# The second layers of an eight-expert block, with the loop over products put outside the loop over experts

## The chip, the cores and the metric

The kernel runs on 1 core of one Trainium2 chip. The metric is device time in microseconds, of which the median of 3 runs is shown. A profile of one execution gives the rows of this document.

## What is computed

A local and a pooled attention give x (2304 tokens by 512); a dense block follows; then a block of eight experts, each token weighted by a matrix P that is balanced over tokens and experts:

```python
h = np.maximum(x @ w_in, 0.0)
x = h * h @ w_out
...
for e in range(E):                     # E = 8
    h = np.maximum(x @ w1[e], 0.0)     # 512 -> 1024
    ye = h @ w2[e]                     # 1024 -> 512
    out += P[:, e:e + 1] * ye
```

All is in float32.

## The kernel before

All instructions are written by generators that an ordering loop (class `Order`) runs against estimated costs; the order in which it takes them is the order of each engine's queue, and each queue runs in that order. All loads and stores are issued by SP, in one queue. Buffers are rings of tiles; a generator that asks for a tile (`get`) waits until one is put back.

Both layers of the experts use seven products instead of eight for a two-by-two split of each matrix multiplication: tokens are taken in three pairs of blocks `pb` of 2 x 384, and the weight and the hidden matrix in halves. Sums and differences of quarters of the weights, and of the hidden matrix, are multiplied. Each float32 operand is split into a high and a low part (`split2`, lines 464 to 468: ScalarE writes the high part at line 466, VectorE or GpSimd the low part at line 468), and a product takes three matmuls of 128x384.

The first layers (`l1_second`, line 1376 for the matmuls) leave, for each expert and pair, the seven hidden combinations in DRAM (`scr_h`). Six units of expert 0 are computed before P is known; they are stored raw (`scr_c`), and `later` (lines 1499 to 1542) loads them in the second layers, multiplies them by P on VectorE (line 1527), forms the combinations (line 1532) and stores them. `later` starts at step 7 of the second layers and goes on by one step for each of its DMAs (`PACE`). Expert 0 is therefore the last of `EXPERTS`.

The second layers are 168 steps (`l2_second`, lines 1608 to 1632): for each expert, each pair and each product, in this order, 24 matmuls into two banks (line 1624). `hidden_loads` (1588) loads each hidden combination in two halves of 384 KB (tiles r); `hidden` (1601) splits a half into a tile of the ring `s_h` (tiles xa, h, i). `l2_weights` (1549) loads the four quarters of an expert's weights once, forms four sums (1575, 1582) and splits seven operands into the ring `s_w` (tiles w, v, u). `collect` (1638) adds each of a step's two banks to an accumulator in SBUF: for the first expert a copy by ScalarE (1647), for the others an add by VectorE (1651). There are 21 accumulators, one for each pair and product. After the last expert `finish` (1655) combines a pair's seven accumulators by seven adds (1663), transposes them (1679), copies them (ScalarE, 1681) and stores 768 KB for each block (1685).

`room` (1191 to 1223) hands out SBUF as the first layers release it: to `s_h` one, four and one tiles, to `s_raw` four.

## Time and profile before

| | |
|---|---|
| median of 3 runs | 2044.64 us (2039.79 to 2044.87) |
| the profiled execution, its own time | 2043.14 us |
| its span, first to last instruction | 2041.4 us |
| mean granted TensorE clock | 0.983 |
| TensorE matmul, VectorE, ScalarE, GpSimd busy | 96%, 76%, 44%, 31% |
| mean DMA rate over the span | 219 GB/s |

PE is TensorE's matmuls, PEld its weight loads, DVE VectorE, ACT ScalarE, POOL GpSimd, SP the engine that issues the DMAs. An "L" and a number is a line of the kernel. In the chain that ended last, each piece is what released the next.

### The profile page before, as it was taken

The page shows a single profiled execution, that of the slowest core. Times are in us where ns is not written, and L with a number is a line of the kernel's source. Part 1 is how long each engine was busy: PE and PEld are TensorE (multiplying, and loading weights), DVE is VectorE, ACT ScalarE, POOL GpSimd, SP SyncE. Part 2 cuts the span into 40 slices and gives each one's busy share as a digit, 9 for nine tenths or more (in the row PEclk, how much of TensorE's full clock was granted, in tenths as well). Part 3 has the DMA queues.
Part 4 walks back from the last instruction along what each step waited for, and adds up shares of the span by engine and source line. Part 5 has one row for each costly group of instructions (what it writes and reads, how often), then busy time and mean ns, then how long its engine had stood idle before and what let it go on. Part 6 is the DMA issues. An engine that isn't in the chain of part 4 may idle for free.

```text
span 2041.4 us, 30758 instructions
## 1 busy us (share of the span) xinstructions
PE 1964.4 (96%) x11201; PEld 1853.8 (91%) x11201; DVE 1542.9 (76%) x2157; ACT 891.6 (44%) x1601; POOL 626.2 (31%) x416
## 2 busy tenths in 40 slices
PE   8899999999989999999999999899999999999997
PEld 5577777899979999999999999898988999999997
DVE  7998988681264777777777777868878787978885
ACT  4575545566633222222222222664434454444543
POOL 4444031002003333333333332023333352534441
PEclk8899999999989999999999999999999999999998
DMA  7667676566475666666666666887876767577664
GB/s 211 213 228 221 209 203 195 157 217 209 138 258 181 234 224 222 234 226 227 224 237 227 218 243 224 300 262 224 248 239 203 269 213 250 179 226 227 194 202 139
DMA packets 244848, 446.84 MB, mean 219 GB/s; under 512 B 22440, under 2 KB 144856, under 8 KB 244696
## 3 DMA queue, kind: packets, MB, share of 16 engines
q1 hardware_dynamic: 244696, 444.87, 67.1%
q8 instruction: 88, 1.44, 0.3%
q14 instruction: 64, 0.52, 0.1%
HBM read 280.61 MB, written 164.18 MB: 218 GB/s over the span
## 4 chain that ended last, share of the span: by engine, by line
PE 79%; DVE 9%; DMA 7%; issue 2%; ACT 2%; POOL 1%; SPq 1%; DVEq 0%; ACTq 0%; POOLq 0%
PE b L1376 33%; PE b L1624 31%; PE b L992 6%; PE b L1033 6%; DMA o<-in_w_in_dram 1%; DMA r<-scr_h 1%; DMA lk<-in_kp_dram 1%; DVE f L922 1%; DVE xa L468 1%; DVE f L924 1%; DVE lp L851 1%; DMA x<-scr_x 1%; DMA o<-in_w_out_dram 1%; DMA lk<-in_vp_dram 0%; DMA xa<-scr_x 0%
## 5 line engine op out<-in xcount | busy, mean ns | idle before, releaser
L1376 PE MATMUL b<-x,w 128*128 128x384 f32 x2688 | 497.4, 338 | 6.3 <-DMA x<-scr_x 5.3
L1376 PEld LDWEIGHTS b<-x,w 128*128 128x128 f32 x2688 | 469.6, 188 | 7.9 <-issue 5.0
L468 DVE TENSOR_TENSOR xa<-r,xa 128x768 fp32r<-128x768 f32 x210 | 260.3, 1253 | 63.1 <-ACT xa L466 62.4
L466 ACT ACTIVATE xa<-r 128x768 fp32r<-128x768 f32 x224 | 189.5, 846 | 243.5 <-DMA r<-scr_h 136.1
L1624 PE MATMUL b<-xa,w 128*128 128x384 f32 x1232 | 263.4, 337 | 5.4 <-DVE xa L468 5.4
L1376 PE MATMUL b<-xa,w 128*128 128x384 f32 x1344 | 263.7, 339 | 3.0 <-DMA xa<-scr_x 3.0
L1376 PEld LDWEIGHTS b<-xa,w 128*128 128x128 f32 x1344 | 238.5, 190 | 4.6 <-DMA xa<-scr_x 3.7
L1624 PEld LDWEIGHTS b<-xa,w 128*128 128x128 f32 x1232 | 219.6, 189 | 6.8 <-DVE xa L468 6.7
L468 POOL TENSOR_TENSOR w<-w,w 128x1024 fp32r<-128x1024 f32 x71 | 158.6, 2234 | 191.8 <-ACT w L466 191.7
L1624 PE MATMUL b<-xa,u 128*128 128x384 f32 x736 | 186.6, 337 | 3.1 <-DVE xa L468 3.1
L1443 ACT ACTIVATE b<-b 128x384 f32<-128x384 f32 x96 | 45.6, 475 | 322.2 <-PE b L1376 320.5
L1624 PE MATMUL b<-xa,v 128*128 128x384 f32 x720 | 167.9, 342 | 5.7 <-DVE v L468 5.7
L1449 ACT ACTIVATE q<-b 128x384 f32<-128x384 f32 x192 | 93.5, 491 | 180.0 <-PE b L1376 149.6
L1033 PE MATMUL b<-g,s 128*128 128x512 f32 (+1 forms) x756 | 168.9, 369 | 0.9 <-ACT t L1058 0.9
L1033 PEld LDWEIGHTS b<-g,s 128*128 128x128 f32 x756 | 135.9, 188 | 17.9 <-ACT t L1058 1.5
L1230 POOL TENSOR_TENSOR w<-w 128x256 f32<-128x256 f32 x64 | 55.0, 859 | 309.3 <-PE b L1376 258.7
L992 PE MATMUL b<-x,s 128*128 128x512 f32 (+1 forms) x600 | 138.7, 374 | 4.8 <-DVE g L1011 3.8
L1624 PEld LDWEIGHTS b<-xa,u 128*128 128x128 f32 x736 | 134.0, 188 | 4.0 <-DVE xa L468 4.0
L1624 PEld LDWEIGHTS b<-xa,v 128*128 128x128 f32 x720 | 131.7, 192 | 6.1 <-DVE v L468 6.1
L1409 DVE SCALAR_TENSOR_TENSOR q<-q,gp 128x768 f32<-128x768 f32 x90 | 125.1, 1390 | 3.1
L1473 DVE TENSOR_TENSOR q<-b,q 128x384 f32<-128x384 f32 x96 | 53.5, 557 | 95.9 <-PE b L1376 95.8
L992 PEld LDWEIGHTS b<-x,s 128*128 128x128 f32 x600 | 107.8, 190 | 20.0 <-DVE g L1011 5.0
(255 smaller groups left out, 3296.5 us busy)
## 6 DMA issues: line engine op xcount, KB each, us to landing
r<-scr_h SPq DMA_DIRECT2D x336, 384.0 KB
scr_h<-q SPq DMA_DIRECT2D x90, 576.0 KB
scr_h<-q SPq DMA_DIRECT2D x180, 192.0 KB
scr_h<-q SPq DMA_DIRECT2D x90, 384.0 KB
s<-scr_w SPq DMA_DIRECT2D x85, 256.0 KB
w<-in_w_dram SPq DMA_DIRECT2D x64, 256.0 KB
gp<-scr_p SPq DMA_DIRECT2D x30, 384.0 KB
m<-scr_w SPq DMA_DIRECT2D x43, 256.0 KB
```

Source lines behind the costliest of these rows:

```text
L466: A.activation(out=hi, in_=x, func=AF.Copy)
L468: eng.tensor_tensor(out=lo_, in0=x, in1=hi.bitcast(F32), op=ALU.subtract)
L851: V.tensor_tensor(out=pr.rearrange("p r s d -> p (r s) d"), in0=sc[:, i].unsqueeze(2).to_broadcast([128, r * W, D]), in1=_free(v[:, :, :], ...
L992: PE.matmul(ps[:, 0:n], lhsT=w[:, a, c], rhs=x[:, b, 0:n], start=(cc == 0 and i == 0), stop=(cc == 3 and i == 2))
L1033: PE.matmul(acc[dc][:, 0:n], lhsT=w[:, a, c], rhs=g[:, b, 0:n], start=(fc == 0 and i == 0), stop=(fc == NF - 1 and i == 2))
L1230: eng.tensor_tensor(out=out, in0=in0, in1=in1, op=op)
L1376: PE.matmul(bank[:, 0:TN], lhsT=w[a][:, iw % 4, cc * 128:cc * 128 + 128], rhs=x[:, b, cc], start=(first and cc == 0 and i == 0), stop=(cc ...
L1409: V.scalar_tensor_tensor(out=x, in0=x, scalar=0.0, in1=p.unsqueeze(1).to_broadcast([128, 2, TN]), op0=ALU.max, op1=ALU.mult)
L1443: A.activation(out=ps[1][:, 0:TN], in_=ps[0][:, 0:TN], func=AF.Copy)
L1449: A.activation(out=c[:, place], in_=ps[bank][:, 0:TN], func=AF.Copy)
L1473: V.tensor_tensor(out=c[:, 2], in0=ps[0][:, 0:TN], in1=c[:, 2], op=ALU.add)
L1624: PE.matmul(ps[d][:, 0:TN], lhsT=w[a][:, q, d * 128:d * 128 + 128], rhs=h[:, b, q % 2], start=(q == 0 and m == 0), stop=(q == NQ - 1 and m ...
```

## The change

Products become the outer loop and experts the inner one. The 168 steps stay; their order is a table, `PASSES`: products 1, 2 and 4 (`PUT_OFF`) for experts 1 to 7 and all pairs; then products 1, 2 and 4 for expert 0; then products 5, 6, 3 and 7 for all eight experts. The products of all experts of one pair are added up in the two banks of that pair, so that six banks are held through a product. `collect` runs once for each pair and product (for the first three products a second time, for expert 0), and adds the banks into two accumulator blocks `u` and `c` of the pair, or straight into an output block, which `turned` transposes, copies and stores in two pieces (256 KB and 128 KB); `finish` is gone.

Weights are loaded for each product and expert: one quarter for products 1, 2 and 4, two for 5 and 7, three for 6, one for 3. The sum formed for product 5 and the one formed for product 6 are stored to DRAM (`scr_s`) and loaded again for products 6 and 3. The sums and low parts of the weights go to GpSimd less readily (1000 ns instead of 3000). `later` starts at step 2, goes on by two steps at fewer places, and not beyond step 50. The ring `s_h` gets five tiles and five more of `s_q`; `s_raw` gets the three tiles of `s_p` when `later` is through; `s_w` gets 18 tiles instead of 19.

```diff
-PRODUCTS = (1, 2, 4, 6, 5, 3, 7)
+PRODUCTS = (1, 2, 4, 5, 6, 3, 7)
-PACE = 1
+PUT_OFF, PACE = (1, 2, 4), 2
 ...
-        s_w.add(slots(p, 4, [128, 4, 256], "u"))
-        s_h.add(slots(p, 1, [128, 4, TN], "i"))
-        s_acc.add(slots(p, 3, [128, 4, TN], "y"))
+        s_w.add(slots(p, 3, [128, 4, 256], "u"))
+        s_h.add(slots(p, 5, [128, 4, TN], "i"))
         yield ("need", lambda: not any(gleft.values()) and len(s_q.idle) == NX2)
-        s_acc.add(s_q)
+        s_h.add(*s_q.all)
+        yield ("need", lambda: len(s_p.idle) == NP2)
+        s_raw.add(*s_p.all)
 ...
-        yield ("need", lambda: at2["step"] >= 7)
+        yield ("need", lambda: at2["step"] >= 2)
-            n = at2["step"] + PACE
+            n = min(at2["step"] + PACE, 50)
 ...
+    PASSES = [(k, pb, e) for k in PUT_OFF for e in EXPERTS[:-1] for pb in range(NPB)]
+    PASSES += [(k, pb, LAST) for k, pb in ((1, 0), (1, 1), (2, 0), (1, 2), (2, 1), (2, 2))]
+    PASSES += [(k, pb, LAST) for k in PUT_OFF[2:] for pb in range(NPB)]
+    PASSES += [(k, pb, e) for k in rest for e in EXPERTS for pb in range(NPB)]
+    TERMS = {1: ((0, 0),), 2: ((1, 0),), 4: ((1, 1),), 5: ((0, 1), (1, 1)), 6: ("S1", (0, 0), (1, 0)), 3: ("S4",),
+             7: ((0, 1), (0, 0))}
 ...
     def l2_weights():
-        for e in EXPERTS:
-            for d, f in ((0, 0), (0, 1), (1, 1), (1, 0)):
-                dma(out=a[f, d], in_=w12[e, f:NF2:2, :, 1, d * 256:(d + 1) * 256].rearrange("q p c -> p q c"))
+        for k, e in WEIGHTS:
+            for term in TERMS[k]:
+                x = yield get(s_w)
+                if (term, e) in scr_s:
+                    dma(out=x, in_=scr_s[term, e])
+                else:
+                    dma(out=x, in_=w12[e, f:NF2:2, :, 1, d * 256:(d + 1) * 256].rearrange("q p c -> p q c"))
+            order.add(weight2(e, k, a, hi, lo_), 8.0)
+    def weight2(e, k, a, hi, lo_):
+        late = 0.0 if k == PRODUCTS[0] else 1000.0
 ...
+        if k == 5:
+            yield from two(x, x, a[1], ALU.add)
+            yield from keep("S1", x)
+        elif k == 6:
+            yield from two(x, x, a[1], ALU.subtract)
+            yield from two(a[2], a[2], x, ALU.subtract)
+        elif k == 7:
+            yield from two(x, a[1], x, ALU.subtract)
+        yield from split2(x, NQ * 256, hi, lo_, late)
+        if k == 6:
+            yield from keep("S4", a[2])
 ...
     def l2_second():
+        for k, pb, e in PASSES:
+            first, last = e == EXPERTS[0] or more and not on, e == LAST or k in PUT_OFF and e == EXPERTS[-2]
 ...
+                            PE.matmul(ps[pb][d][:, 0:TN], lhsT=w[a][:, q, d * 128:d * 128 + 128], rhs=h[:, b, q % 2],
+                                      start=(first and q == 0 and m == 0), stop=(last and q == NQ - 1 and m == 2),
+                                      skip_group_check=True)
+            if last:
+                order.add(collect(pb, k, ps[pb], more), 1.2)
 ...
+    def collect(pb, k, ps, more):
+        for d in range(2):
+            if k == 1 and not more:
+                A.activation(out=u[:, d], in_=ps[d][:, 0:TN], func=AF.Copy)
+            for x, of in adds:
+                V.tensor_tensor(out=x[:, d], in0=ps[d][:, 0:TN], in1=of[:, d], op=ALU.add)
+            for x, of, _, _ in outs:
+                V.tensor_tensor(out=x[:, d], in0=ps[d][:, 0:TN], in1=x[:, d] if of is None else of[:, d], op=ALU.add)
+    def turned(x, t0, d0):
+        for t, n in ((0, 2), (2, 1)):
+                    PE.transpose(ps[:, i * 256 + d * 128:i * 256 + d * 128 + 128], x[:, d, c], ident)
+            dma(out=out[t0 + t * 128:t0 + (t + n) * 128, d0:d0 + 256].rearrange("(t p) d -> p t d", p=128), in_=o[:, t:t + n])
```

Three places show how the change moves instructions. The first is VectorE's queue in the early second layers. Before, from the second expert on (xa, i, h on line 468 are low parts of hidden halves, b a bank, xa on line 1651 an accumulator):

```order
L468 TENSOR_TENSOR xa_1973_13656<-r_1969_13625,xa_1973_13656 128x768
L468 TENSOR_TENSOR xa_1978_13680<-r_1970_13634,xa_1978_13680 128x768
L1651 TENSOR_TENSOR xa_1820_12809<-b_1974_13657,xa_1820_12809 128x384
L1651 TENSOR_TENSOR xa_1820_12809<-b_1975_13663,xa_1820_12809 128x384
L468 TENSOR_TENSOR i_1980_13698<-r_1972_13648,i_1980_13698 128x768
L468 TENSOR_TENSOR h_1987_13723<-r_1976_13671,h_1987_13723 128x768
L1651 TENSOR_TENSOR xa_1820_12809<-b_1981_13699,xa_1820_12809 128x384
L1651 TENSOR_TENSOR xa_1820_12809<-b_1985_13707,xa_1820_12809 128x384
L468 TENSOR_TENSOR xa_1990_13742<-r_1979_13690,xa_1990_13742 128x768
L468 TENSOR_TENSOR xa_1994_13764<-r_1986_13714,xa_1994_13764 128x768
L1651 TENSOR_TENSOR xa_1836_12896<-b_1991_13743,xa_1836_12896 128x384
L1651 TENSOR_TENSOR xa_1836_12896<-b_1992_13748,xa_1836_12896 128x384
```

Now, in the first product (u and w are low parts of weights):

```order
L468 TENSOR_TENSOR i_1805_12796<-r_1804_12786,i_1805_12796 128x768
L468 TENSOR_TENSOR i_1807_12807<-r_1806_12797,i_1807_12807 128x768
L468 TENSOR_TENSOR q_1809_12818<-r_1808_12808,q_1809_12818 128x768
L468 TENSOR_TENSOR u_1812_12830<-w_1802_12771,w_1811_12829 128x1024
L468 TENSOR_TENSOR h_1814_12854<-r_1810_12826,h_1814_12854 128x768
L468 TENSOR_TENSOR xa_1816_12865<-r_1815_12855,xa_1816_12865 128x768
L468 TENSOR_TENSOR xa_1818_12875<-r_1817_12866,xa_1818_12875 128x768
L468 TENSOR_TENSOR xa_1820_12889<-r_1819_12876,xa_1820_12889 128x768
L468 TENSOR_TENSOR w_1823_12901<-v_1813_12831,v_1822_12900 128x1024
L468 TENSOR_TENSOR q_1825_12912<-r_1821_12894,q_1825_12912 128x768
```

The two adds of each step are gone from between the splits, and low parts of weights stand there instead.

The second place is SP's queue about step 112 of 168 (r and gp are raw hidden halves, w, v and u weight tiles, scr_S the weight sums in DRAM). Before:

```order
L1598 DMA r_2538_16892<-scr_h_0_161 128x768
L1598 DMA r_2545_16926<-scr_h_0_161 128x768
L1598 DMA r_2546_16936<-scr_h_1_162 128x768
L1598 DMA r_2553_16968<-scr_h_1_162 128x768
L1598 DMA r_2556_16983<-scr_h_1_162 128x768
L1567 DMA u_2558_16991<-in_w_dram 128x4x256
L1598 DMA r_2560_17012<-scr_h_1_162 128x768
L1598 DMA r_2565_17030<-scr_h_1_162 128x768
L1567 DMA w_2561_17014<-in_w_dram 128x4x256
```

Now, while products of kind 6 are multiplied:

```order
L1581 DMA u_2388_16490<-in_w_dram 128x4x256
L1627 DMA r_2391_16517<-scr_h_0_161 128x768
L1597 DMA scr_S_7_182<-v_2365_16348 128x1024
L1627 DMA r_2395_16537<-scr_h_1_162 128x768
L1578 DMA w_2397_16542<-scr_S_1_176 128x1024
L1627 DMA r_2399_16564<-scr_h_1_162 128x768
L1578 DMA v_2402_16569<-scr_S_2_177 128x1024
L1627 DMA gp_2404_16586<-scr_h_2_163 128x768
L1627 DMA gp_2407_16608<-scr_h_2_163 128x768
L1597 DMA scr_S_0_175<-u_2388_16490 128x1024
```

The loads of weights stand closer, and stores and loads of weight sums stand between the hidden loads; the last store shown writes the tile that the first row loads.

The third place is the end of VectorE's queue. Before, after the last product's matmuls (q are accumulators):

```order
L1651 TENSOR_TENSOR q_1914_13314<-b_2943_19299,q_1914_13314 128x384
L1651 TENSOR_TENSOR q_1914_13314<-b_2945_19305,q_1914_13314 128x384
L1663 TENSOR_TENSOR q_1862_13057<-q_1862_13057 128x768
L1663 TENSOR_TENSOR q_1879_13143<-q_1862_13057,q_1879_13143 128x768
L1663 TENSOR_TENSOR q_1879_13143<-q_1879_13143 128x768
L1663 TENSOR_TENSOR q_1862_13057<-q_1879_13143,q_1898_13230 128x768
L1663 TENSOR_TENSOR q_1898_13230<-q_1862_13057,q_1898_13230 128x768
L1663 TENSOR_TENSOR q_1898_13230<-q_1862_13057,q_1914_13314 128x768
L1663 TENSOR_TENSOR q_1879_13143<-q_1879_13143,q_1914_13314 128x768
```

Now (i are two output blocks, b the last two banks):

```order
L1697 TENSOR_TENSOR i_2720_18953<-b_2645_18215,xa_1890_13300 128x384
L1697 TENSOR_TENSOR i_2721_18954<-b_2645_18215,xa_1890_13300 128x384
L1697 TENSOR_TENSOR i_2720_18953<-b_2646_18221,xa_1890_13300 128x384
L1697 TENSOR_TENSOR i_2721_18954<-b_2646_18221,xa_1890_13300 128x384
```

Of the last step's two adds from banks and seven sums, four adds from banks are left.

## Rows read from the trace of the kernel before

**Rows 1.** Page, busy time by engine over the span
```profile
PE 1964.4 (96%) x11201; PEld 1853.8 (91%) x11201; DVE 1542.9 (76%) x2157; ACT 891.6 (44%) x1601; POOL 626.2 (31%) x416
```

**Rows 2.** Page, the chain that ended last, by line
```profile
PE b L1376 33%; PE b L1624 31%; PE b L992 6%; PE b L1033 6%; DMA o<-in_w_in_dram 1%; DMA r<-scr_h 1%; DMA lk<-in_kp_dram 1%; DVE f L922 1%; DVE xa L468 1%; DVE f L924 1%; DVE lp L851 1%; DMA x<-scr_x 1%; DMA o<-in_w_out_dram 1%; DMA lk<-in_vp_dram 0%; DMA xa<-scr_x 0%
```

**Rows 3.** Stretches: us, then PE, PEld, DVE, ACT, POOL busy (xinstructions), PEclk, DMA share, GB/s
```profile
1280.00:1320.00 40.00, 34.27 (x180) 33.67 (x179) 34.49 (x41) 24.79 (x36) 0.00 (x0) 0.91 0.83 284
1320.00:1380.00 60.00, 60.00 (x347) 60.00 (x346) 38.35 (x36) 40.00 (x61) 13.29 (x5) 1.00 0.85 270
1380.00:1420.00 40.00, 34.92 (x185) 33.30 (x185) 34.93 (x38) 15.81 (x21) 16.99 (x6) 0.96 0.66 211
...
1480.00:1520.00 40.00, 35.83 (x202) 34.68 (x201) 30.69 (x38) 15.45 (x18) 15.96 (x7) 1.00 0.69 220
...
1560.00:1620.00 60.00, 52.72 (x286) 50.78 (x285) 49.45 (x57) 22.94 (x28) 21.67 (x9) 0.97 0.66 220
...
1700.00:2000.00 300.00, 300.00 (x1731) 299.78 (x1730) 246.56 (x279) 144.41 (x171) 122.59 (x49) 1.00 0.69 212
```

**Rows 4.** Waits of PE, 1285:2025 us
```profile
PE b L1624 <- DVE xa L468: 8.5, 7, 3.3
PE b L1624 <- DVE v L468: 5.7, 1, 5.7
```

**Rows 5.** Chain in order of time, 1272:1680 us: start us, us, what
```profile
1283.46 5.78 DMA r<-scr_h
...
1292.18 0.95 DVE h L468
1293.13 1.15 DVE v L468
```

**Rows 6.** The same view, 1380:1420 us
```profile
1392.52 0.56 DVE y L1651 x2
...
1395.02 2.26 DVE xa L468
...
1399.03 5.23 DVE xa L468 x2
...
1404.28 3.44 DMA r<-scr_h
...
1409.69 2.37 POOL w L468
```

**Rows 7.** DVE and POOL groups, 1700:2000 us: xcount | busy us, mean ns | idle before
```profile
L468 DVE TENSOR_TENSOR xa<-r,xa 128x768 fp32r<-128x768 f32 x87 | 116.6, 1357 | 23.4 <-ACT xa L466 23.0
...
L1651 DVE TENSOR_TENSOR q<-b,q 128x384 f32<-128x384 f32 x60 | 31.1, 551 | 14.3 <-PE b L1624 14.3
...
L468 POOL TENSOR_TENSOR w<-w,w 128x1024 fp32r<-128x1024 f32 x5 | 12.9, 2572 | 9.4 <-ACT w L466 9.4
```

**Rows 8.** Line 468, 1620:2010 us: duration ns min/median/max, first and last start
```profile
L468 DVE TENSOR_TENSOR xa<-r,xa x113: 939/957/3153, 1619.6 to 2008.2; 128x768 fp32r<-128x768 f32 x113
```

**Rows 9.** DVE groups, 1295:1400 us
```profile
L468 DVE TENSOR_TENSOR w<-w,w 128x1024 fp32r<-128x1024 f32 x1 | 1.2, 1226 | 0.0
```

**Rows 10.** Saturated and mixed stretches of the DMA engines, columns as in Rows 3
```profile
1276.00:1290.00 14.00, 12.59 (x72) 11.99 (x70) 13.02 (x19) 7.51 (x10) 0.00 (x0) 1.00 1.05 402
1266.00:1276.00 10.00, 10.00 (x59) 10.00 (x58) 6.32 (x11) 1.94 (x5) 0.00 (x0) 1.00 1.00 307
1320.00:1336.00 16.00, 16.00 (x95) 16.00 (x94) 7.87 (x11) 10.38 (x16) 0.00 (x0) 1.00 1.01 355
```

**Rows 11.** Order of time at the end
```profile
2024.14 1.08 DVE L1651 TENSOR_TENSOR q<-b,q 128x384 f32<-128x384 f32 x2 [3.97 <-PE b L1624]
...
2031.60 3.93 PE L1679 MATMUL b<-ident,q 128*128 128x128 f32 x22 [5.02 <-DVE q L1663]
2032.33 0.60 ACT L1681 ACTIVATE xa<-b 128x512 f32<-128x512 f32 x1 [9.67 <-PE b L1679]
...
2034.03 2.24 ACT L1681 ACTIVATE xa<-b 128x512 f32<-128x512 f32 x4 [0.26 <-PE b L1679]
```

More of the change, by code (lines that the diff above doesn't have):

```diff
@@ L1546, in tile_kernel @@
     hk, ev_hk = {}, {(e, pb, k): [Event(), Event()] for e in range(E) for pb in range(NPB) for k in PRODUCTS}
-    acc, ev_acc = {}, {(e, pb, k): [Event(), Event()] for e in range(E) for pb in range(NPB) for k in PRODUCTS}
+    accs, c11, before = {}, {}, {pb: [] for pb in range(NPB)}
+    ev_last = {pb: [Event(), Event()] for pb in range(NPB)}
+    rest = [k for k in PRODUCTS if k not in PUT_OFF]
+    LAST = EXPERTS[-1]
+    PASSES = [(k, pb, e) for k in PUT_OFF for e in EXPERTS[:-1] for pb in range(NPB)]
@@ new lines, in l2_second @@
+        ps = {}
+        for k, pb, e in PASSES:
+            at2["step"] += 1
+            more = k in PUT_OFF and e == LAST
+            on = k == 2 and more
+            first, last = e == EXPERTS[0] or more and not on, e == LAST or k in PUT_OFF and e == EXPERTS[-2]
+            if on:
+                yield ("wait", *ev_last[pb])
+            elif first:
+                ps[pb] = []
+            yield ("wait", ev_w2[e, k])
+            w = w2[e, k]
+            for i in range(2):
+                yield ("wait", ev_hk[e, pb, k][i])
+                h = hk.pop((e, pb, k, i))
+                for q in range(2 * i, 2 * i + 2):
+                    for d in range(2):
+                        if q == 0 and len(ps[pb]) <= d:
+                            ps[pb].append((yield get(b_q)))
+                        yield _pe_r(TN)
+                        for m, (a, b) in enumerate(((0, 0), (0, 1), (1, 0))):
+                            PE.matmul(ps[pb][d][:, 0:TN], lhsT=w[a][:, q, d * 128:d * 128 + 128], rhs=h[:, b, q % 2],
+                                      start=(first and q == 0 and m == 0), stop=(last and q == NQ - 1 and m == 2),
+                                      skip_group_check=True)
+                s_h.put(h)
+            if pb == NPB - 1:
+                s_w.put(*w2.pop((e, k)))
+            if last:
+                order.add(collect(pb, k, ps[pb], more), 1.2)
@@ new lines, in collect @@
+    def collect(pb, k, ps, more):
+        if k == 1 and not more:
+            accs[pb] = yield get(s_acc)
+        yield ("wait", *before[pb])
+        before[pb] = [Event()]
+        done = before[pb][0]
+        u, c = accs[pb][:, 0:2], accs[pb][:, 2:4]
+        outs = []
+        if k == 2 and more:
+            outs = [(c11.pop(pb), None, 0, 0)]
+        else:
+            for to in {2: ((0, 0),), 3: ((1, 0),), 7: ((1, 1), (0, 1))}.get(k, ()):
+                x = yield get(s_h, F32, [128, 2, TN])
+                outs.append((x, c if to == (0, 1) else u, *to))
+        adds = {1: ((u, u), (c, c)) if more else (), 2: (), 4: ((c, c) if more else (c, u),), 5: ((u, u),),
+                6: ((u, u), (c, c)), 3: (), 7: ()}[k]
+        for d in range(2):
+            if k == 1 and not more:
+                yield _b(TN)
+                A.activation(out=u[:, d], in_=ps[d][:, 0:TN], func=AF.Copy)
+            for x, of in adds:
+                yield _w(TN)
+                V.tensor_tensor(out=x[:, d], in0=ps[d][:, 0:TN], in1=of[:, d], op=ALU.add)
+            for x, of, _, _ in outs:
+                yield _w(TN)
+                V.tensor_tensor(out=x[:, d], in0=ps[d][:, 0:TN], in1=x[:, d] if of is None else of[:, d], op=ALU.add)
+            if not (k == 1 and more):
+                b_q.put(ps[d])
+            else:
+                order.fire(ev_last[pb][d])
+        order.fire(done)
+        for x, _, nh, low in outs:
+            if k == 2 and not more:
+                c11[pb] = x
+            else:
+                order.add(turned(x, (2 * pb + nh) * TN, low * 256), 1.5)
```

157 lines of the change are left out of this document (49 added, 108 removed).

## Prediction

> **What bounds the kernel now.** I read the page first: TensorE is busy 96% of the span, VectorE 76%, GpSimd 31% [rows 1], and the chain that ended last runs a third of the span through the first-layer products (line 1376) and another 31% through the second-layer products (line 1624) [rows 2]. The change rewrites only the second-layer part, so the question is not how busy TensorE is on average but how much of that part it loses. The stretches answer it. From 1700 to 2000 us TensorE starts 1731 matmuls in 300 us, 0.1733 us each, at full clock [rows 3]; that is the price of a matmul with nothing in its way, 4.16 us for a step of 24. Against that rate, 40 us should hold 231 and 60 us 346. The stretch 1320:1380 holds 347: nothing lost. 1280:1320 holds 180 (51 missing, 8.8 us), 1380:1420 185 (46, 7.9 us), 1480:1520 202 (29, 5.0 us), 1560:1620 286 (60, 10.4 us) [rows 3]. Together 32.1 us, part of it at a granted clock of 0.91 to 0.97. Between those holes, and from 1620 on, the part is at TensorE's rate. After the last product there is a tail: VectorE takes over at 2024.1 [rows 11] and the span ends at 2041.4, 17.3 us later. So 49 us are within reach, and no more, because the number of matmuls stays.
>
> What makes the holes? The waits of PE name VectorE's split of the hidden tiles ("xa L468", 8.5 us in 7 waits) and one split of weights ("v L468", 5.7 us in one) [rows 4]. The chain shows the first hole as a hidden load of 5.78 us, then a split of h and last the split of the weights of the third product, 1.15 us [rows 5]. In the second hole VectorE's splits follow each other, 2.26 and 5.23 us for three, then a load of 3.44 us and a late weight split of 2.37 us on GpSimd [rows 6]. VectorE is 82% busy even in the quiet stretch (246.56 of 300 us) [rows 3], partly because a split of 128x768 takes 957 ns by the median but 1357 ns on the mean, up to 3153, beside GpSimd's weight splits of 2572 ns [rows 7, 8].
>
> **The change part by part.** The order gives the counts, the rows the prices; the sum is made against the profiled execution, 2043.1 us (its span and 1.7 us around it), which lies 1.5 us under the median shown.
>
> TensorE: 168 steps of 24 matmuls and 72 transposes before and after: nothing.
>
> VectorE: 294 adds of 128x384 from the banks go, and 72 come in their place; 222 fewer at 0.551 us [rows 7] are 122 us. 18 adds of 128x768 at the end go, about 17 us at 0.957. From GpSimd come 46 weight splits and 24 weight sums at 1.226 us [rows 9], 86 us, and 21 hidden splits at 0.957, 20 us [rows 8]. Net 33 us less over 700 us. GpSimd is nearly empty then, so a split should cost its median: 129 splits of the quiet stretch at 957 instead of some 1360 ns are 52 us per 300. VectorE comes out near 60% there (247 less 52 less 14 of 300). None of this is on the path by itself; it works through the holes.
>
> The order of VectorE matters more than its load. Before, every step puts two adds that wait for that very step into VectorE's queue, and the next splits stand behind them. In the new order no add from a bank stands between the splits for 21 steps on end (24 later). The first expert of the old kernel is the natural trial: its sums are copied by ScalarE, so its 21 steps have no such adds, and the stretch 1320:1380, which also carries the gating of a deferred unit, loses nothing [rows 3]; the second hole begins at 1392, where VectorE's adds of the second expert stand in the chain for the first time [rows 6]. The rings grow as well: 15 tiles for split hidden halves instead of 6, and 7 raw ones instead of 4 once the deferred units are through; full, that is 11 steps or 46 us of cover. I therefore take the three later holes, 23.3 us, to go whole (bounds 0 and 23.3).
>
> The first hole stays in part. Its hidden loads come through the same queue behind the same stores. Of its end the weight split goes (1.15 us [rows 5]; steps 1 to 3 now share one weight), and one 0.52 MB load fewer stands ahead of the first hidden load, 1.3 us at 402 GB/s [rows 10]. 8.8 less 2.5 leaves 6.3 us (bounds 3 and 9).
>
> Deferred units: the same instructions, begun at step 2 instead of 7, to be done by step 64 instead of about 147. In the first 66 steps SP issues 83 MB, 303 GB/s at 275 us; 355 GB/s is shown in a stretch of the same mix, 1320:1336, without a lost matmul (95 in 16 us) [rows 10]. I cost it at nothing; its cover is the ring, and a late store would hold up the fourth step of the last expert first.
>
> DMA: 56 more weight loads and 16 stores of 0.52 MB, 38 MB. They crowd: in steps 73 to 112 SP issues 80 hidden loads, 34 weight loads, 15 sum stores and 6 output pieces, 58.3 MB in 166 us, 350 GB/s. The trace shows 402 GB/s in 14 us of full engines, 355 with a mix like this one, and 307 in a stretch rich in weight loads, whose packets are the shortest [rows 10]. At 402 or 355 nothing is late; at 307 the block takes 190 us, 24 us late, inside a full cover of 46. I take 355, the nearest mix: nothing (bounds 0 and 24).
>
> Here a page stands against the change. The Trainium skill, HBM Reference, Specifications, puts a core's effective share of HBM at about 358 GB/s. It holds for the average of this block, but two pieces of eight steps want 382 and 378, some 2 us late each, which would make the sum 4 us longer if nothing covered them. The trace does not show such a ceiling (402 over 14 us), and the same page says that a core streaming alone gets more, so the measurement decides.
>
> The tail: before, two adds, seven sums of 128x768 in a row, transposes from 2031.6, six copies by ScalarE to 2036.3, and the last store and end 5.1 us after that [rows 11]. After: four adds of 128x384, 2.2 us, of which the first half can start as the first bank stops, 0.5 us before the last matmul; then as before 1.4 us from the last add to the end of the first copy; three more copies at the pitch of 0.85 us (2032.33 to 2034.03 is two of them [rows 11]) or less, 2.4 us; and a last store of 128 KB instead of 768, which I take 1.6 us shorter by its bytes at 402 GB/s [rows 10], 3.5 us. Sum 9.0, with some queueing of the twelve stores 9.3: 8.0 us less (bounds 6.5 and 9).
>
> Sum: 2043.1 less 2.5, 23.3 and 8.0 is **2009 us**, 1.7% less. What is late next is TensorE itself.
>
> **The rivals.** *The later holes have other causes* and the change does not do what it is for: the deferred units' loads, gating and stores stand in the same queues and are now packed into fewer steps. For it: the splits in the second hole stand beside gating, and a load of 3.44 us follows [rows 6]. Against: the loss-free stretch with gating. If half of the 23.3 us stays: 2021; if all: 2032. Chance 0.13.
>
> *DMA bounds steps 73 to 112.* If the short weight packets and the traffic both ways pull the rate to 270 GB/s, the block takes 216 us, 50 late; with half of the cover filled, 27 us reach TensorE: 2036. Against: in no full stretch was the rate below 307 [rows 10]. Chance 0.10, half of it below 2037.
>
> *Slower: the sum stores block SP's queue.* Each of the 15 stores of weight sums there waits in SP's queue for an add, which waits for its weight load; every hidden load behind it waits too. If each held the queue for a landing (5.78 us [rows 5]) and an add (1.226 us [rows 9]), 15 of them are 105 us; less a cover of 46, 59 us reach TensorE: 2068. It turns the result to slower from 82 us in all (46 of cover and the 36 gained, with 2), 5.5 us a store. Against: in the order the store stands 2.5 to 19 steps behind its load, and the closest, 2.5 steps, is 10.4 us, more than 7. Chance 0.09.
>
> **How the numbers follow.** My forecast has 0.68 and its own range 2001 (all holes gone, the short tail) to 2020. 0.3%, 6 us, is about what a measurement of this kernel can tell from no change. Faster by more: the forecast, the first rival whole and half of the second, 0.86. Within it: most of the rest of the second, 0.04. Slower: the third and what little the second adds, 0.10. Up to 2031 the range takes in most of the first rival and a part of the second, 0.8 in all: 2001 to 2031.
>
> **What would show it.** Right: after the first hole every stretch to the end has 5.77 matmuls per us; VectorE near 60 to 70% and GpSimd near idle there; split hidden tiles at a mean near 960 ns; waits of PE on line 468 only at the start; a tail near 9 us. Wrong: holes 90 to 200 us after the part's start (the deferred units), or about 300 to 470 us after it with DMA share near 1 (bandwidth) or with SP waiting for VectorE and DMA share low (the queue); a start hole over 9 us; a price per matmul other than 0.1733 us.

## The result and the profile after

The changed kernel takes 2013.74 us (median of 4 runs, 2010.96 to 2016.88) against 2043.51 us for the kernel before (4 runs, 2039.79 to 2044.87). The ratio is 0.9858, 95% interval 0.9837 to 0.9878, so 1.4% less. The profiled execution took 2010.96 us, its span is 2009.2 us and its mean granted clock 0.987.

The page's busy times by engine answer to [rows 1]:

```profile
PE 1955.2 (97%) x11201; PEld 1849.7 (92%) x11201; DVE 1411.5 (70%) x2010; ACT 877.9 (44%) x1569; POOL 386.7 (19%) x322
```

VectorE's busy time fell by 131 us and GpSimd's by 240 over the span, while TensorE executes the same 11201 matmuls. As before, that says little about the time; the stretches do (same columns as [rows 3]):

```profile
1280.00:1320.00 40.00, 39.36 (x225) 38.65 (x224) 29.53 (x39) 18.49 (x23) 0.00 (x0) 1.00 0.99 353
1320.00:1380.00 60.00, 60.00 (x347) 60.00 (x346) 44.32 (x51) 38.56 (x48) 0.00 (x0) 1.00 0.96 327
1380.00:1420.00 40.00, 40.00 (x231) 40.00 (x230) 25.57 (x26) 21.52 (x26) 0.00 (x0) 1.00 0.92 307
1480.00:1520.00 40.00, 40.00 (x232) 40.00 (x231) 22.09 (x27) 15.10 (x19) 0.00 (x0) 1.00 0.94 312
1520.00:1560.00 40.00, 34.62 (x199) 34.30 (x197) 27.91 (x37) 17.58 (x21) 1.80 (x1) 0.98 1.00 347
1560.00:1620.00 60.00, 58.72 (x324) 58.06 (x325) 44.18 (x55) 29.30 (x39) 9.66 (x4) 0.93 0.92 321
1620.00:1660.00 40.00, 40.00 (x232) 40.00 (x231) 31.72 (x32) 21.86 (x26) 0.00 (x0) 1.00 0.99 357
1660.00:1700.00 40.00, 40.00 (x231) 40.00 (x230) 32.45 (x35) 19.39 (x23) 2.42 (x1) 1.00 0.99 360
1700.00:2000.00 300.00, 300.00 (x1739) 299.79 (x1738) 169.76 (x186) 130.67 (x156) 4.79 (x2) 1.00 0.71 227
```

At 231 matmuls in 40 us and 346 in 60, the first stretch now misses 6 (1.0 us) where it missed 51, and the stretches of the old second and third hole are full. But a hole stands where there was none: 1520:1560 misses 32 and 1560:1620 still 22, 54 matmuls or 9.4 us together, part of it at a granted clock of 0.93. From there to the end nothing is lost, also at 1620 to 1700 us, where the DMA engines are busy 0.99 of the time at 357 and 360 GB/s.

The waits of PE, 1260 to 2010 us (us in total, times, longest), in place of [rows 4]:

```profile
PE b L1660 <- DVE xa L1694: 6.7, 2, 5.8
PE b L1660 <- DVE i L468: 0.6, 1, 0.6
PE b L1718 <- DVE i L1697: 0.5, 1, 0.5
```

No wait on a split is left except one of 0.6 us. The one large wait is for adds from the banks (line 1694). The order of time about it, 1553 to 1566 us (start us, us, engine, line, operation; in brackets the idle time before and what ended it), shows what stood ahead of those adds in VectorE's queue:

```profile
1556.31 2.15 DVE L1593 TENSOR_TENSOR u<-u,w 128x1024 f32<-128x1024 f32 x1 [3.43 <-DMA w<-in_w_dram]
1558.39 0.55 DVE L1694 TENSOR_TENSOR xa<-b,xa 128x384 f32<-128x384 f32 x1
...
1560.41 0.98 PE L1660 MATMUL b<-q,u 128*128 128x384 f32 x2 [5.79 <-DVE xa L1694]
```

VectorE stood still for 3.43 us before the third weight sum of product 5, which waited for its weight load; the first two had run at 1508.1 and 1534.0 us. Behind it in the queue stood the adds that must read product 1 of the last expert from a pair's banks before product 2 is added on top of it there. TensorE needed those adds at once, for step 66; the sum belongs to the third expert of product 5, whose first step is the 79th, some 54 us later. The load is a piece of the chain (start us, us, what):

```profile
1549.74 6.55 DMA w<-in_w_dram
```

Low parts and adds in the quiet stretch, VectorE's groups from 1700 to 2000 us, answer to [rows 7]:

```profile
L468 DVE TENSOR_TENSOR xa<-r,xa 128x768 fp32r<-128x768 f32 x23 | 22.0, 957 | 13.9 <-ACT xa L466 13.7
L468 DVE TENSOR_TENSOR q<-gp,q 128x768 fp32r<-128x768 f32 x21 | 21.3, 1013 | 15.7 <-ACT q L466 15.7
```

The group xa<-r takes 957 ns on the mean where it took 1357, and all 129 splits of hidden halves in the stretch 967 where as many took 1358; GpSimd runs only two instructions there (4.79 us). VectorE is busy 57% of the stretch, where it was 82% [rows 3].

The end, in order of time, answers to [rows 11]:

```profile
2001.24 1.95 DVE L1697 TENSOR_TENSOR i<-b,xa 128x384 f32<-128x384 f32 x4 [1.06 <-PE b L1660]
2001.40 0.34 PE L1660 MATMUL b<-xa,u 128*128 128x384 f32 x1
...
2002.78 1.45 PE L1718 MATMUL b<-ident,i 128*128 128x128 f32 x11 [0.50 <-DVE i L1697]
...
2003.37 0.60 ACT L1722 ACTIVATE xa<-b 128x512 f32<-128x512 f32 x1 [0.71 <-PE b L1718]
...
2004.60 0.40 ACT L1722 ACTIVATE q<-b 128x256 f32<-128x256 f32 x1
...
2005.51 0.40 SPq L1727 DMA_DIRECT2D out_dram<-q  x1
```

The span ends at 2009.2, 7.8 us after the last product's matmul starts; before it was 17.1 (2024.3 to 2041.4). The adds are done at 2003.19 and the last copy at 2005.0.

**Where the 32.2 us of span went.** The first matmul of the second layers starts at 1280.7 us (before: 1282.6), the last at 2001.4 (2024.3). So 1.9 us lie ahead of the part that was changed, 21.0 in it (741.7 to 720.7 us from first to last start) and 9.3 in the tail. In the part, the first hole gives 7.8 us; the three later ones, 23.3 us, are replaced by one of 9.4; the 0.7 us by which that is more than 21.0 is spread.

### The profile page after: what moved, and what is told of

The parts are those of the page before. It is cut to its first block, busy times and chain, and to the rows that moved or that the text cites. A ratio compares the mean times of both kernels' runs of the same rounds, so it can differ in the third digit from the quotient of the medians.

```text
span 2009.2 us, 30685 instructions
## 1 busy us (share of the span) xinstructions
PE 1955.2 (97%) x11201; PEld 1849.7 (92%) x11201; DVE 1411.5 (70%) x2010; ACT 877.9 (44%) x1569; POOL 386.7 (19%) x322
## 4 chain that ended last, share of the span: by engine, by line
PE 74%; DVE 11%; DMA 9%; issue 2%; ACT 2%; SPq 1%; POOL 0%; DVEq 0%; ACTq 0%; POOLq 0%
PE b L1377 34%; PE b L1660 27%; PE b L992 6%; PE b L1033 5%; DMA r<-scr_h 4%; DMA o<-in_w_in_dram 1%; DVE lp L798 1%; DVE f L922 1%; DVE f L924 1%; DVE lp L851 1%; DMA lk<-in_kp_dram 1%; DVE g L1011 1%; DMA scr_h<-gp 1%; DVE ls L807 1%; DVE q L468 1%
## 5 line engine op out<-in xcount | busy, mean ns | idle before, releaser
L1377 PE MATMUL b<-xa,w 128*128 128x384 f32 x1344 | 263.7, 338 | 3.3 <-DMA xa<-scr_x 3.3
L1377 PEld LDWEIGHTS b<-xa,w 128*128 128x128 f32 x1344 | 238.5, 190 | 5.0 <-DMA xa<-scr_x 4.1
L468 POOL TENSOR_TENSOR w<-w,w 128x1024 fp32r<-128x1024 f32 x64 | 140.8, 2200 | 179.0 <-ACT w L466 179.0
L1660 PE MATMUL b<-i,w 128*128 128x384 f32 x664 | 156.5, 338 | 0.6 <-DVE i L468 0.6
L1660 PE MATMUL b<-q,w 128*128 128x384 f32 x672 | 156.1, 336 | 0.0
L1660 PE MATMUL b<-xa,w 128*128 128x384 f32 x560 | 129.5, 335 | 0.0
L1463 DVE SCALAR_TENSOR_TENSOR q<-b,gp 128x384 f32<-128x384 f32 x180 | 100.1, 556 | 30.7 <-PE b L1377 26.6
L1660 PEld LDWEIGHTS b<-q,w 128*128 128x128 f32 x672 | 120.7, 189 | 0.0
L1660 PEld LDWEIGHTS b<-i,w 128*128 128x128 f32 x664 | 119.1, 188 | 0.9 <-DVE i L468 0.8
L1660 PE MATMUL b<-i,v 128*128 128x384 f32 x472 | 118.6, 336 | 0.0
L1660 PE MATMUL b<-q,v 128*128 128x384 f32 x464 | 115.3, 336 | 0.0
```

Of the source, the lines that this page charges most:

```text
L468: eng.tensor_tensor(out=lo_, in0=x, in1=hi.bitcast(F32), op=ALU.subtract)
L1377: PE.matmul(bank[:, 0:TN], lhsT=w[a][:, iw % 4, cc * 128:cc * 128 + 128], rhs=x[:, b, cc], start=(first and cc == 0 and i == 0), stop=(cc ...
L1463: V.scalar_tensor_tensor(out=c[:, i], in0=ps[bank][:, 0:TN], scalar=0.0, in1=p[:, 0], op0=ALU.max, op1=ALU.mult)
L1660: PE.matmul(ps[pb][d][:, 0:TN], lhsT=w[a][:, q, d * 128:d * 128 + 128], rhs=h[:, b, q % 2], start=(first and q == 0 and m == 0), stop=(las ...
```

## The experiments

One caution first. The start of the second layers, up to which the two kernels do the same, lies between 1277.1 and 1294.5 us in the profiles of this study. So I read from each profile the time from the first to the last start of a second-layer matmul ("second layers"), with the waits, beside the times of all runs. That measure leaves the tail out, and it comes from one profile of each kernel: a_ring6 and a_nosum below, whose edits turn out to change little, lie 6.1 and 3.5 us under the changed kernel, so differences of that size are not told apart. Ratios are to the kernel before, run on the same chip. "b" variants are edits of the kernel before, "a" variants of the changed one.

| run | median us (runs) | ratio, 95% interval | second layers us |
|---|---|---|---|
| before | 2043.51 (4) | 1 | 741.7 |
| changed | 2013.74 (4) | 0.9858, 0.9837 to 0.9878 | 720.7 |
| b_noadd | 2032.60 (9) | 0.9937, 0.9917 to 0.9956 | 731.0 |
| b_copy | 2038.14 (10) | 0.9979, 0.9962 to 0.9996 | 736.2 |
| b_nogate | 2023.67 (4) | 0.9899, 0.9859 to 0.9939 | 718.4 |
| a_dummy | 2033.98 (10) | 0.9953, 0.9935 to 0.9971 | 736.7 |
| a_ring6 | 2016.78 (4) | 0.9868, 0.9830 to 0.9905 | 714.6 |
| a_wlate | 2018.42 (4) | 0.9885, 0.9851 to 0.9920 | 724.8 |
| a_nosum | 2014.51 (4) | 0.9856, 0.9814 to 0.9899 | 717.2 |
| a_pool | 2011.40 (4) | 0.9842, 0.9794 to 0.9890 | 713.2 |
| a_nogate | 2008.61 (5) | 0.9819, 0.9795 to 0.9844 | 710.6 |
| a_dose | 2080.56 (4) | 1.0173, 1.0148 to 1.0199 | 782.5 |
| a_pool2 | 2008.04 (5) | 0.9843, 0.9817 to 0.9870 | 714.0 |
| a_dose2 | 2023.91 (6) | 0.9911, 0.9884 to 0.9937 | 728.2 |

### Were the old holes the adds' fault?

The forecast took the later holes away because the per-step adds go. **b_noadd** takes only the adds from the kernel before:

```diff
         if e == EXPERTS[0]:
             yield _b(TN)
             A.activation(out=o, in_=ps[:, 0:TN], func=AF.Copy)
-        else:
-            yield ("wait", ev_acc[EXPERTS[EXPERTS.index(e) - 1], pb, k][d])
-            yield _w(TN)
-            V.tensor_tensor(out=o, in0=ps[:, 0:TN], in1=o, op=ALU.add)
```

> The kernel before, with collect copying the first expert's banks only: the 294 adds of the other experts on VectorE are left out (the output holds one expert). Theory A (the per-step adds on VectorE make the later holes): the three later holes, 23 us, go, the first hole (8.8 us) and most of the 17 us tail stay: 2018 to 2024 us. Theory B (the deferred units make the holes): under 6 us change, 2037 us or more.

Stretches and waits of PE in b_noadd, after the first stretch in the kernel before:

```profile
1380.00:1440.00 60.00, 54.92 (x300) 53.30 (x300) 49.27 (x59) 25.00 (x31) 16.99 (x6) 0.97 0.76 249
```

```profile
1380.00:1440.00 60.00, 55.13 (x302) 54.49 (x301) 34.86 (x33) 25.91 (x32) 15.72 (x6) 0.94 0.79 257
...
1480.00:1520.00 40.00, 36.31 (x199) 35.67 (x198) 21.66 (x25) 16.06 (x20) 12.83 (x5) 0.96 0.77 236
...
1560.00:1620.00 60.00, 59.92 (x342) 59.29 (x341) 45.18 (x38) 28.09 (x33) 22.37 (x8) 1.00 0.83 268
```

```profile
PE b L1624 <- ACT w L466: 4.9, 2, 3.0
PE b L1624 <- POOL w L468: 1.8, 1, 1.8
PE b L1624 <- POOL v L468: 1.8, 1, 1.8
```

The time, 2032.6 us, lies in neither theory's range. Without any add, the second hole (44 missing, before 46) and the third (32, before 29) are there in full; only the fourth closes. The waits change hands: no longer hidden splits [rows 4], but parts of the next expert's weights, from ScalarE and GpSimd. The second layers gain 10.7 us, not 23.3. And VectorE is busy only 58% of the stretch 1380:1440 (34.86 of 60), so neither adds nor a full VectorE explain that hole.

**b_copy** keeps the traffic from the banks but gives it to ScalarE (every expert's banks are copied as the first one's were):

```diff
-        if e == EXPERTS[0]:
-            yield _b(TN)
-            A.activation(out=o, in_=ps[:, 0:TN], func=AF.Copy)
-        else:
-            yield ("wait", ev_acc[EXPERTS[EXPERTS.index(e) - 1], pb, k][d])
-            yield _w(TN)
-            V.tensor_tensor(out=o, in0=ps[:, 0:TN], in1=o, op=ALU.add)
+        yield _b(TN)
+        A.activation(out=o, in_=ps[:, 0:TN], func=AF.Copy)
```

> The kernel before, with each step's two banks copied by ScalarE instead of added by VectorE for every expert (the adding up over experts is left out). Theory A in its first form (VectorE's load and its queue): as without the adds, 2018 to 2024 us. Theory A in its second form (any instruction that waits for a step's end and stands among the splits holds them, on ScalarE as on VectorE): holes stay, 2032 us or more. Theory B: 2037 us or more.

Half of that gain is lost again (736.2 us), with PE waiting 7.6 us for ScalarE's high parts of weights: its copies now stand in the same queue, likely ahead of them.

**b_nogate** is the first rival's cause. The deferred units are the six units of expert 0 that `later` finishes; their eight VectorE operations each (four multiply by P, the gating proper, and four form combinations; I call all eight the gating) go, while loads and stores stay. Two of the stores take another tile, since the one that they read is no longer written.

```diff
-        for x, g in ((c[0][:, 0], 0), (c[0][:, 1], 1), (c[1][:, 0], 1), (c[1][:, 1], 0)):
-            yield _w2(TN)
-            V.scalar_tensor_tensor(out=x, in0=x, scalar=0.0, in1=p[:, g], op0=ALU.max, op1=ALU.mult)
 ...
-            yield _w2(TN)
-            V.tensor_tensor(out=out, in0=in0, in1=in1, op=op)
```

> The kernel before, with the eight VectorE operations of each deferred unit left out (its stored values are stored again as they are); loads, stores and pacing stay. Theory A: a hole or two get smaller, 2033 to 2043 us. Theory B: the three later holes go, 2018 to 2024 us.

```profile
1280.00:1320.00 40.00, 33.95 (x183) 33.32 (x182) 36.13 (x42) 25.46 (x36) 0.00 (x0) 0.91 0.87 298
...
1380.00:1440.00 60.00, 60.00 (x346) 60.00 (x346) 45.66 (x53) 27.91 (x34) 19.02 (x7) 1.00 0.90 289
...
1480.00:1520.00 40.00, 39.49 (x226) 39.17 (x225) 33.25 (x39) 16.94 (x20) 13.46 (x5) 1.00 0.88 291
...
1560.00:1620.00 60.00, 60.00 (x345) 60.00 (x344) 51.19 (x57) 28.19 (x34) 21.94 (x9) 1.00 0.74 231
```

All three later holes close, but for 5 matmuls at 1480:1520, with every add in place, and VectorE is busier (45.66 us) in 1380:1440 than in b_noadd. The first hole stays. The second layers gain 23.3 us, just what the forecast had put on the adds. So the old later holes need the gating; the adds make them worse (the fourth hole needs both).

The edit takes away two things at once, the operations and what the first of each unit waits for at the head of VectorE's queue. In the kernel before, VectorE's waits from 1320 to 1620 us hold this one:

```profile
DVE gp L1527 <- DMA gp<-scr_p: 8.8, 4, 3.5
```

VectorE stands idle for the load of P, 3.51 us up to 1380.7, 2.04 up to 1492.8 and 2.06 up to 1551.4, and TensorE's first wait in each of the three holes begins 3 to 17 us later. The fourth such wait (1.15 us, 1441.7) is followed by no hole. No run separates these waits from the operations.

### What keeps them away in the changed kernel?

The changed kernel still has all six deferred units. **a_dummy** gives VectorE load back, four idle operations per step that wait for no matmul:

```diff
+            if at2["step"] > 1:
+                order.add(extra(), 1.2)
 ...
+    def extra():
+        x = lg.rearrange("p t e -> p (t e)")
+        for _ in range(4):
+            yield _w2(NTT * E)
+            V.tensor_tensor(out=x, in0=x, in1=x, op=ALU.max)
```

> The changed kernel with four idle VectorE operations of 128x144 in each of 167 steps, which wait for nothing, some 1.2 us a step or 200 us in all: the load of the old adds without their waits. If VectorE's load was what mattered: holes come back, 2026 us or more. If the waits for the step mattered: within 5 us of the changed kernel, 2010 to 2019 us.

```profile
1440.00:1480.00 40.00, 36.32 (x205) 36.01 (x204) 31.68 (x68) 14.87 (x17) 2.40 (x1) 0.96 0.70 224
...
1520.00:1560.00 40.00, 37.17 (x208) 35.96 (x207) 34.84 (x69) 16.96 (x20) 2.78 (x1) 1.00 1.00 347
1560.00:1620.00 60.00, 48.41 (x274) 47.18 (x273) 53.45 (x92) 24.41 (x31) 20.43 (x8) 0.91 0.81 266
...
1700.00:2000.00 300.00, 298.80 (x1721) 298.27 (x1720) 264.68 (x492) 138.41 (x165) 20.12 (x8) 1.00 0.78 259
```

```profile
PE b L1662 <- DVE i L468: 13.3, 3, 11.5
PE b L1662 <- DVE q L468: 4.5, 2, 3.7
```

With VectorE busy 88% of 1700:2000 (82% in the kernel before), the waits for hidden splits are back and 16.0 us are lost, most of it before 1620 us, while the deferred units run or have just ended. The load of VectorE counts, although these operations wait for no step: the forecast's sentence that the order of VectorE matters more than its load is not borne out. The largest wait, 11.5 us up to 1575.9, is for a split behind eight idle operations in a row. They took 9.35 us there, from 1565.6, though one takes 0.30 us by the median, while GpSimd was at work on weights; so over half of the loss lies at one place, where the load was slowed beside GpSimd. After 1700 us the same load costs 3.1 us (1721 matmuls in 300 us, 1739 in the changed kernel).

**a_ring6** keeps one of the forecast's two grounds away: split hidden halves get the old six tiles, the other tiles serve the output blocks alone.

```diff
-            s_h.add(slots(p, 5, [128, 4, TN], "i"))
+            s_h.add(slots(p, 1, [128, 4, TN], "i"))
 ...
-        s_h.add(*s_q.all)
+        s_o.add(*s_q.all)
```

> The changed kernel with the old ring of 6 tiles for split hidden halves instead of 15 (output blocks take tiles of their own). If the larger ring is what carries TensorE over the deferred units' waits (theory C): the later holes come back, 2023 us or more. If spreading weights and taking the adds out of the steps is enough without it (theory D): within 5 us of the changed kernel, 2009 to 2019 us.

No hole comes back: from 1320 to 1560 us nothing is lost, 1560:1620 misses 10 matmuls, and the second layers are 6 us shorter than in the changed kernel's profile. The time is no lower, because in this profile they start 8.0 us later (1288.7) and the tail is 4.6 us longer (12.4). The larger ring is not what closes the holes.

### What is the new hole?

The ordering loop shifts other instructions a little with every edit below, so I count matmuls missing from 1520 to 1620 us (577 when full): 54 in the changed kernel, but 11 in a_ring6 and 29 in a_nosum (below), whose edits leave VectorE's work there as it is. One profile tells 54 from none, but not 11 from 29.

**a_wlate** moves product 5's weight loads behind the deferred units, so that no sum of weights stands in VectorE's queue ahead of the adds at 1558 us:

```diff
         for k, e in WEIGHTS:
+            if k == rest[0]:
+                yield ("need", lambda: at2["step"] >= 67)
```

> The changed kernel, with the weight loads of product 5 held back until step 67. If the hole of 9 us at 1550 to 1570 us is VectorE waiting, ahead of the last expert's adds, for a weight load of product 5: most of it goes, 2002 to 2008 us. If it is the full DMA engines that make the hidden halves late: no gain, 2010 to 2018 us.

The wait on the adds goes, but 74 matmuls are missing at product 5's own start, for its weights, and the time, 2018.4 us, is no gain:

```profile
PE b L1662 <- DVE v L468: 7.9, 1, 7.9
PE b L1662 <- ACT w L466: 3.3, 1, 3.3
```

**a_nosum** takes away the sixteen stores of weight sums and everything that waits for them (the raw quarter is loaded in their place):

```diff
-    ... 6: ("S1", (0, 0), (1, 0)), 3: ("S4",),
+    ... 6: ((0, 1), (0, 0), (1, 0)), 3: ((1, 0),),
 ...
-            yield from keep("S1", x)
 ...
-            yield from keep("S4", a[2])
```

> The changed kernel without the 16 stores of weight sums: products 6 and 3 load a raw quarter of the same size in place of each stored sum, so the loads stay, and the sums they stand for are left out. If the stores and SP's waits for them cost nothing, as forecast: within 4 us of the changed kernel, 2010 to 2018 us. If they hold SP's queue: 2006 us or less.

The time is the changed kernel's (0.9856 against 0.9858), and 29 are missing in the place of the hole. The stores and SP's waits for them cost nothing that can be seen.

**a_pool** and **a_pool2** hand weight work back to GpSimd as readily as the old kernel did, for all products, or only for 2, 4 and 5:

```diff
-        late = 0.0 if k == PRODUCTS[0] else 1000.0
+        late = 0.0 if k == PRODUCTS[0] else LATE
```

```diff
-        late = 0.0 if k == PRODUCTS[0] else 1000.0
+        late = 0.0 if k == PRODUCTS[0] else LATE if k in (2, 4, 5) else 1000.0
```

> The changed kernel with the old preference of 3000 ns for GpSimd in the weight sums and low parts: 70 or so of them of 128x1024 go back from VectorE to GpSimd. If VectorE's load decides where holes come: the hole at 1550 us shrinks and the time is 2005 to 2011 us. If contention of the two eats the gain: within 4 us of the changed kernel or above it, 2010 to 2020 us.

> The changed kernel with the work on weights sent to GpSimd more readily (the old 3000 ns instead of 1000) for products 2, 4 and 5 alone, where the deferred units load VectorE; products 6, 3 and 7 as in the changed kernel. Theory that VectorE's load before product 5 makes the hole: it shrinks from 9 us to 0 to 4, time 2003 to 2010 us. Rival, that splits on GpSimd slow VectorE's own splits and come later by 1.3 us each: hole as large or larger, time 2012 to 2020 us.

The hole has 4 and 14 missing matmuls, the second layers take 713.2 and 714.0 us. a_pool2 has the lowest median of the runs that compute all of the block, 2008.0 us, but both intervals overlap the changed kernel's, and a_ring6 has 11 missing and 714.6 us without this edit: that the edit shrinks the hole is not shown. a_pool has GpSimd busy 48.9 us from 1320 to 1560, beside the gating, and 95.66 of the 300 us from 1700 on, and TensorE is busy throughout: in the changed kernel GpSimd's weight work makes no hole by itself. It does slow VectorE's splits again (VectorE's groups, 1700 to 2000 us, one of eight; all 132 splits have a mean of 1336 ns):

```profile
L468 DVE TENSOR_TENSOR xa<-r,xa 128x768 fp32r<-128x768 f32 x22 | 30.5, 1387 | 14.7 <-ACT xa L466 14.5
```

**a_nogate** is b_nogate's edit made in the changed kernel.

> The changed kernel without the eight VectorE operations of each of the six deferred units (the gating by P and the four combinations are left out of what is computed; their loads, stores and order stay). Theory that VectorE's work for the deferred units, packed into the first 50 steps, is what makes product 5's first weight sum late: the hole of 9 us at 1555 to 1562 us is gone, 1520 to 1560 us holds 231 matmuls and 1560 to 1620 us 346, and the time is 2003 to 2006 us. Rival, that the hole is the 6.55 us landing of a weight load behind the last deferred stores on full DMA engines: the hole stays at 6 to 9 us and the time at 2010 to 2014 us.

```profile
1520.00:1560.00 40.00, 40.00 (x232) 39.96 (x231) 33.83 (x39) 19.09 (x23) 10.72 (x4) 1.00 0.96 333
1560.00:1620.00 60.00, 59.98 (x349) 59.57 (x348) 45.09 (x53) 32.18 (x42) 5.61 (x2) 1.00 0.97 336
```

No matmul is missing, with the DMA engines as full as before, and PE waits 0.8 us in all. The median, 2008.6 us, lies between the two ranges. The second layers take 710.6 us, 10.1 less; the times agree (0.9819 against 0.9858, some 8 us, though the two intervals touch). But a_ring6, with the gating, is only 4.0 us behind. So the gating costs 4 to 10 us in the changed kernel, 23.3 in the old one. VectorE still waits 3.9 us, in 2 waits between 1320 and 1620 us, for weight loads of its sums, and nothing is lost by it: such a wait alone is no hole. How the gating comes to make the load late, or its order to stand so badly, was not traced.

### How near are the DMA engines to the bound?

**a_dose** issues the 32 weight loads of products 5 and 6 that come from the weights twice:

```diff
                     dma(out=x, in_=w12[e, f:NF2:2, :, 1, d * 256:(d + 1) * 256].rearrange("q p c -> p q c"))
+                    if k in (5, 6):
+                        yield _dma(128 * 4096)
+                        dma(out=x, in_=w12[e, f:NF2:2, :, 1, d * 256:(d + 1) * 256].rearrange("q p c -> p q c"))
```

> The changed kernel with the direct weight loads of products 5 and 6 issued twice, 32 loads of 0.52 MB or 16.8 MB more between about step 60 and step 112. Theory that DMA has room up to its 402 GB/s and the rings cover the rest: the block of steps 73 to 112 wants 75 MB, 187 us at 402 GB/s, about 21 us late against a cover of 46 us; the stretches 1620 to 1700 us stay full to within 5 us, the hole at 1555 us grows by one load or two (2 to 5 us), time 2012 to 2020 us. Rival, that the block is already at the limit of about 358 GB/s: each extra byte is paid, 16.8 MB are 47 us, 10 to 46 of them on TensorE, time 2023 to 2060 us, with missing matmuls at 1600 to 1720 us and a DMA share of 1.0 beside them.

It is by far the slowest run, and neither theory's picture fits: beside the holes the engines are not full. Stretches, and SP's waits, 1285 to 2080 us:

```profile
1560.00:1620.00 60.00, 37.54 (x206) 36.15 (x204) 31.97 (x44) 21.92 (x29) 2.42 (x1) 0.85 0.85 284
1620.00:1660.00 40.00, 35.52 (x191) 35.52 (x192) 16.30 (x16) 9.97 (x12) 0.00 (x0) 0.89 0.76 258
```

```profile
SPq L1584 <- DMA w<-in_w_dram: 82.3, 17, 6.2
SPq L1584 <- DMA u<-in_w_dram: 27.6, 5, 6.6
SPq L1584 <- DMA v<-in_w_dram: 26.6, 6, 5.7
```

The second load writes the tile of the first, so SP waits until the first has landed: 28 waits, 136.5 us, 4.9 us each, with every later load behind them. The run was meant to weigh bytes and weighed the queue too: together they lengthen the second layers by 62 us. **a_dose2** moves the same bytes without a tile to wait for, into DRAM tiles that nobody reads:

```diff
+            if k in (5, 6):
+                for d in range(2):
+                    y = dr.tile([128, NQ, 256], F32, name=f"dose_{k}_{e}_{d}")
+                    yield _dma(128 * 4096)
+                    dma(out=y, in_=w12[e, 0:NF2:2, :, 1, d * 256:(d + 1) * 256].rearrange("q p c -> p q c"))
```

> The changed kernel with 32 more transfers of 0.52 MB, 16.8 MB, beside the weight loads of products 5 and 6, as the run a_dose, but from DRAM into unused DRAM tiles, so that no instruction and no queue waits for any of them. The run a_dose took 2080.6 us (70 us more than the changed kernel), and in it SP waited 121 us in 25 waits for its second load of the same tile. Theory that those waits of SP made the 70 us, and that DMA bytes alone are cheap: 16.8 MB at 402 GB/s are 42 us of engine time, of which the rings and the room beside 345 GB/s (1560 to 1720 us) cover most: 2013 to 2025 us. Rival, that the DMA engines were full already (share 0.99 and 358 GB/s from 1585 to 1725 us in the changed kernel) and every byte is paid: 16.8 MB at 358 GB/s are 47 us, 2040 to 2065 us, with DMA share 1.0 beside missing matmuls.

```profile
1560.00:1620.00 60.00, 50.75 (x278) 49.74 (x277) 40.35 (x52) 27.09 (x35) 0.00 (x0) 0.89 1.00 356
1620.00:1660.00 40.00, 40.00 (x232) 40.00 (x231) 27.11 (x28) 18.74 (x22) 0.00 (x0) 1.00 1.05 397
1660.00:1700.00 40.00, 37.43 (x204) 36.79 (x204) 27.50 (x28) 18.04 (x21) 0.93 (x1) 0.96 1.05 399
1700.00:1740.00 40.00, 40.00 (x232) 40.00 (x231) 27.86 (x31) 18.42 (x22) 1.48 (x1) 1.00 1.05 400
```

16.8 MB more cost 10 us (7.5 in the second layers). For 120 us the engines move 397 to 400 GB/s and TensorE misses 27 matmuls, 4.7 us, there; the hole ahead of it grows to 69. SP waits a little here too: 6.8 us in 6 waits before it issues one of the new transfers, 6.7 us in 8 that end with one. The bytes are mostly covered; if they cost the same in a_dose, some 54 of its 62 us are left for SP's waits.

## Why the prediction was right, and where it was not

The sign and the size came out: 2009 us forecast, 2013.74 measured, within 2001 to 2031. By its own terms, against the profiled execution:

- **Price per matmul and what is within reach: right.** 1739 matmuls in 300 us, none added; the time came from holes and the tail alone.
- **First hole, −2.5 forecast, −7.8 measured: mis-sized.** The forecast counted from the third product's weight split only its own 1.15 us [rows 5]. The wait on it was 5.7 us [rows 4], and it goes whole: it stays in b_noadd (5.5 us) and b_nogate (5.9 us), and every changed kernel, whose first three steps share one weight, has at least 222 matmuls in the stretch. When an operation disappears, so does the wait for its input.
- **Later holes, −23.3 forecast, −13.9 measured: the failed step.** "The order of VectorE matters more than its load" and "the rings grow as well" were the two grounds. Taking the adds away gives 10.7 us, not 23.3; the small ring brings nothing back; load without waits brings 16.0 us back. The deferred units' gating is the cause without which no later hole forms. That was the first rival's cause, and a part of its consequence came ("half of the 23.3 us stays"): under the lighter VectorE 9.4 us are lost at one place in this profile, less in a_ring6 and a_nosum. The forecast excluded the gating by one loss-free stretch, 1320:1380 [rows 3]. There the gating ran from 1335.0 to 1341.6 us, with no adds in VectorE's queue and GpSimd idle; GpSimd's work on the next expert's weights began at 1357.8. In the second hole, which the forecast dated from the adds at 1392, the gating had stood at the head of VectorE's queue from 1377.2, waiting for P. A stretch that carries one of several loads does not clear that load.
- **VectorE's load: right.** 57% in 1700:2000 where the forecast was near 60, splits at 967 ns on the mean where it had 957.
- **Deferred units cost 0: wrong by 4 to 10 us** (a_nogate). The forecast named the right danger, an in-order queue whose head waits, for the adds alone. At 1556 us it was a weight sum whose load took 6.55 us to land. The place was nearly named: the hole stands before the third step of the last expert, where the forecast feared a late store before the fourth.
- **DMA of steps 73 to 112, cost 0: right.** 358 GB/s was held from 1585 to 1725 us without a lost matmul. The Trainium skill, HBM Reference, Specifications, gives about 358 GB/s as a core's effective share and says that a core streaming alone measures above it; a_dose2 moves 400, so for one busy core the first figure was no ceiling, and the trace agrees with the second statement.
- **Sum stores in SP's queue, cost 0: right** (a_nosum). The rival's mechanism is real and its price was near: 4.9 us a wait in a_dose against the 5.8 taken for a landing. It did not happen because the sums are ready when SP comes to their stores.
- **Tail, −8.0 forecast, −9.3 measured: mis-sized.** The last copy ends 1.8 us after the last add where 3.8 were forecast, because the last transposes begin 0.4 us before the last add ends and the copies follow each other at 0.26 to 0.49 us, not at 0.85. (Measured from the last matmul's start; the forecast's 17.3 and 9.3 were from the adds.)

The errors of the first hole (5.3 us too little) and of the tail (1.3) and that of the later holes (9.4 too much) cancel for the most part. That is luck: the total is a better number than the argument behind its largest term.

**Still open.** That the second and third old hole come 10 to 40 us after a change of expert, when each of seven steps needs a new weight operand, while the new order needs one every third step, fits b_noadd's waits for weights, but no run isolates it. In b_noadd's second hole the chain runs through GpSimd's weight work (splits of 2.46 and 2.38 us and two sums of 6.17 together, 1395.3 to 1409.5 us), and no run takes that off GpSimd in the old kernel, so it may be the load that the gating meets there. Whether the new hole is as large in each execution of the changed kernel I can't say; a_ring6 and a_nosum, with the same work there, miss 11 and 29 matmuls where it misses 54. The 17 us by which the start of the second layers varies were not traced.

## What to carry to other kernels

- Before a hole is booked to one cause, take that cause alone out of the old kernel and look at the stretch: here two loads had to meet, the removal of either shrank the holes, and the gains (10.7 and 23.3 us) don't add.
- In an in-order queue ask what each instruction at the head may wait for, loads included, and who stands behind it. One load of 6.55 us, for a sum that TensorE needed some 54 us later, held up adds that it needed at once.
- Bytes on a nearly full DMA system cost little where rings give cover (16.8 MB, 10 us); waits in the queue that issues them cost more (136.5 us of waits, some 54 us by difference).
